# Column sums by VectorE for part of the score tiles, and a new order at the start of an attention unit

## The chip, the cores and the metric

The kernel runs on one core of one Trainium2 chip. The metric is the device time of that core in microseconds. TensorE (PE in the profile) multiplies, ScalarE (ACT) does the exponentials, VectorE (DVE) the reductions and elementwise work, GpSimd (POOL) some products and a part of the transfers, SyncE (SP) issues the rest.

## The reference

Attention over 8 batches of 12 heads, 448 positions and 64 features, with queries and keys normalised by their root mean square, and then a two-layer MLP over the 3584 tokens:

```python
q_n, k_n = (rmsnorm(q, g_q), rmsnorm(k, g_k))
scores = scale * np.matmul(q_n, k_n.transpose(0, 1, 3, 2))
scores = scores - np.max(scores, axis=-1, keepdims=True)
attn = np.exp(scores)
attn = attn / (np.sum(attn, axis=-1, keepdims=True) + 1e-09)
attn_out = np.matmul(attn, v)
...
x = attn_out.transpose(0, 2, 1, 3).reshape(B * S, H * D)      # 3584 x 768
h = x @ w_in                                                  # 768 x 2048
g = np.maximum(0.01 * h, h)
out = g @ w_out                                               # 2048 x 768
```

## The kernel before

**Units.** A unit is four heads of one batch; there are 24 (`NU`), three to a batch. Scores are kept transposed: keys on the partitions, queries along the free dimension. A unit has seven score tiles of 128 x 896 (`sT`, two PSUM banks each, 448 columns in each bank). For each tile TensorE runs four 64x64 matmuls (`score`, L195), ScalarE one exponential into the fp16 tile `et` (L214). There are two such `sT` slots, taken in turn.

**The loop.** Units 3 to 23 run through four stages `d` each (L928 to L1006): `STEPS` gives stage 0 the score tile 0, and stages 1 to 3 two tiles each. After a stage's scores and exponentials, `fill` (L703) takes MoE items from `queue` and puts them on TensorE: first-layer items (`moe1`, six matmuls of 448 columns, L363), second-layer items (`moe2`, eight of 384 columns, L404), and items of a seven-product scheme for pairs of output tiles (`seven`, L445), whose sums VectorE makes (L426 to L435) and whose banks it evacuates (L452, L461). How many items a stage gets follows from the costs that stand with the items (1.13, 1.31, or 0.575), the weights `WD` and a running `debt`. Small pieces of preparation for later units ("jobs") are placed between the items, one after each, and the rest behind them. Evacuations are put off through `pend` until the next item or the end of the fill (`flush`). Each engine takes its instructions in the order in which they are written here; nothing is scheduled automatically.

**The shift.** Exponentials need a bound. From tile 0 of a unit VectorE takes the maximum of each partition (`shift_max`, L232) and builds a diagonal `dg` (L234); a matmul with ones spreads it over all partitions (`shift_mm`, L244, or L250 for the first units); VectorE takes the maximum of that (L245) and makes the bias `eb` (L253). All exponentials of the unit wait for `eb`.

**Stage 0 of a unit `u`** also finishes unit `u - 1`. For "narrow" units (4 to 22) TensorE runs PV (`pv_slot`, 28 matmuls into the other `sT` slot), the column sums over the keys (`zcol`, 16 matmuls with a 32-column matrix of ones, L283), and then the shift of `u`, into unused columns of the slot that PV has just filled. ScalarE copies PV out (`pv_out`, L295), VectorE folds the sums (`zcol_sum`, L300). `zcol_inv` makes the reciprocal and spreads it by DMA, and GpSimd or VectorE multiplies (`xmul_pool`, `xmul_sb`, L321). Unit 23 and units up to 3 take wide sums instead (`zsum_slot`, 28 matmuls of 64x64, L265).

**Preparation** of unit `u + 2`: sums of squares (L155) in stage 1, the inverse root (L160, L161) and the normalisation (L167) in stage 2. V is loaded as fp16 into one of `NV` buffers by GpSimd's queue (`load_v`, L124).

The lines of stage 0 that the change reorders are L932 to L947.

Of the kernel before, what the change touches and what calls it, by code (L numbers as in the profile page):

```python
# [18 lines left out]
def kernel(  # L19
# [22 lines left out]
    DELTA = 1.0  # L42
    NV = 4

# [194 lines left out]
    def shift_mm(u):  # L239
        s = st[u]  # L240
        if u > 0 and "pslot" in st[u - 1]:
            pb = st[u - 1]["pslot"][:, :, S:S + 64]
            for x in range(2):
# [14 lines left out]
    xts = {}  # L258

    def zsum(u, t0=0, t1=NS):  # L260
        s = st[u]
        for t in range(t0, t1):
            for r in range(2):
                for a in range(2):
                    nc.tensor.matmul(s["zt"][r][64 * a:64 * a + 64, 0:S], ones16[64 * r:64 * r + 64],  # L265
                                     s["et"][64 * r:64 * r + 64, t, a], start=(t == 0), stop=(t == NS - 1))

# [8 lines left out]
    def zcol(u):  # L276
        s = st[u]
        s["zc"] = aux([P, 512], FP32, "zc")
        for i, (t, n) in enumerate(((0, 2), (NS - 1, 1), (2, 2), (4, 2))):
            for y in range(2):  # L280
                for a in range(2):
                    c = 32 * (2 * y + a)
                    nc.tensor.matmul(s["zc"][c:c + 32, 0:n * HS].rearrange("p (k x) -> p k x", k=n), onesr,  # L283
                                     s["et"][:, t:t + n, a, HS * y:HS * y + HS], start=(i == 0), stop=(i == 3))

# [103 lines left out]
    def flush():  # L389
        while pend:  # L390
            pend.pop(0)()
# [305 lines left out]
    def narrow(u):  # L697
        return 4 <= u < NU - 1

    def fed(u, d):  # L700
        return u % NQ == 0 and d == 3

    def fill(u, d, jobs):  # L703
# [11 lines left out]
        while queue and debt[0] >= queue[0][0] * 0.5:  # L715
# [3 lines left out]
            if jobs:  # L719
                jobs.pop(0)()  # L720
        flush()
        for job in jobs:
# [22 lines left out]
    with tc.manual_schedule():  # L745
# [110 lines left out]
        prep_sqp(4, (0,))  # L856
        load_v(4)
        for f in range(2):
# [29 lines left out]
        load(6)  # L888
        gate(3)
        prep_sqp(4, (1,))  # L890
        prep_sqp(5)
        load_v(5)
        qk(2, (2,))
# [34 lines left out]
        for u in range(3, NU):  # L928
            for d in range(4):
                if d > 0 or u > 3:  # L930
                    qk(u, STEPS[d])
                    if d == 0:  # L932
                        shift_max(u)
                        if u == 6:
                            xmul_sb(u - 2)
                        if narrow(u - 1):
                            pv_slot(u - 1)
                            zcol(u - 1)
                            shift_mm(u)
                            pv_out(u - 1)  # L940
                            zcol_sum(u - 1)
                        else:
                            zsum_slot(u - 1)
                            pv(u - 1)
                            shift_mm(u)
                            zinv(u - 1)
                    ex(u)  # L947
# [5 lines left out]
                if d == 0:  # L953
# [8 lines left out]
                    if u + 4 < NU:  # L962
                        job(load, u + 4)
                    if u + 3 < NU:
                        load_v(u + 3)
                    if u < 6:
# [15 lines left out]
                if u + 2 < NU:  # L982
# [3 lines left out]
                    if d == 2:  # L986
                        job(prep_rinv, u + 2)
                        for ti in range(2):
                            job(prep_norm, u + 2, ALL, (ti,))
                        if u > 3:  # L990
                            job(prep_trd, u + 2)
                if d == 1 and 4 <= u < 8:
                    job(weight_sum, u - 4, 0)
                if d == 0 and 5 <= u < 9:
                    job(weight_sum, u - 5, 1)
                if d == 2 and 6 <= u < 8:
                    job(xmul_sb, u - 1)
                if u == NU - 2 and d == 0:
# [47 lines left out]
```

## Time and profile before

| | |
|---|---|
| time, median of 3 runs | 421.86 us (420.86 to 422.32) |
| span of the profiled execution | 419.0 us |
| PE busy | 402.7 us, 96% |
| ACT busy | 304.6 us, 73% |
| DVE busy | 279.5 us, 67% |
| POOL busy | 82.9 us, 20% |
| granted TensorE clock | full in all 40 slices |

Groups that the change touches, with the busy time of the group and the mean of one instruction:

| group | count | busy us | mean ns |
|---|---|---|---|
| L283 PE zc, 448 columns | 216 | 15.3 | 356 |
| L283 PE zc, 224 columns | 72 | 4.8 | 259 |
| L232 DVE maximum of tile 0 | 22 | 24.1 | 1093 |
| L295 ACT copy of PV | 19 | 17.2 | 907 |
| L244 PE shift, 64 columns | 38 | 4.4 | 197 |

Busy times of matmuls overlap, since four small tiles run side by side and matmuls are pipelined; what a group costs on the path is better read from the chain of waits, where each piece has only the time by which it moves the end. "issue" there is time without a visible cause, and "A <- B" in the list of waits means that A's engine stood idle until B was done.

### The profile page before, as it was taken

The page shows a single profiled execution, that of the slowest core. Times are in us where ns is not written, and L with a number is a line of the kernel's source. Part 1 is how long each engine was busy: PE and PEld are TensorE (multiplying, and loading weights), DVE is VectorE, ACT ScalarE, POOL GpSimd, SP SyncE. Part 2 cuts the span into 40 slices and gives each one's busy share as a digit, 9 for nine tenths or more (in the row PEclk, how much of TensorE's full clock was granted, in tenths as well). Part 3 has the DMA queues.
Part 4 walks back from the last instruction along what each step waited for, and adds up shares of the span by engine and source line. Part 5 has one row for each costly group of instructions (what it writes and reads, how often), then busy time and mean ns, then how long its engine had stood idle before and what let it go on. Part 6 is the DMA issues. An engine that isn't in the chain of part 4 may idle for free.

```text
span 419.0 us, 9148 instructions
## 1 busy us (share of the span) xinstructions
PE 402.7 (96%) x3731; PEld 217.6 (52%) x3731; DVE 279.5 (67%) x459; ACT 304.6 (73%) x474; POOL 82.9 (20%) x75
## 2 busy tenths in 40 slices
PE   7787999999999999999999999999999999999995
PEld 7454444544445544454445544454445547558863
DVE  5888675898569736576449746468349788627762
ACT  5999877768887689867986779967986657653600
POOL 1958422200010121210121111120101101010000
PEclk9999999999999999999999999999999999999999
DMA  8999996889664996677665796578554460032023
GB/s 265 239 251 260 237 252 85 219 153 207 163 153 74 216 229 108 166 177 165 158 127 105 201 193 154 152 147 186 159 111 45 119 152 13 2 82 76 2 54 97
DMA packets 71949, 62.39 MB, mean 149 GB/s; under 512 B 36324, under 2 KB 67044, under 8 KB 71908
## 3 DMA queue, kind: packets, MB, share of 16 engines
q1 hardware_dynamic: 61312, 49.62, 47.2%
q0 software_dynamic: 10272, 11.80, 18.1%
q8 instruction: 29, 0.48, 0.4%
q10 hardware_dynamic: 324, 0.39, 0.3%
q14 instruction: 12, 0.10, 0.1%
HBM read 45.61 MB, written 11.01 MB: 135 GB/s over the span
## 4 chain that ended last, share of the span: by engine, by line
PE 83%; ACT 9%; DVE 6%; issue 1%; DVEq 0%; ACTq 0%
PE hps L363 27%; PE sT L195 8%; PE sT L341 6%; ACT et L214 6%; PE ma L445 5%; PE md L445 5%; PE mc L445 5%; PE bank L445 5%; PE bank L565 4%; PE op L404 3%; PE zc L283 3%; PE mb L445 3%; PE warm L743 2%; PE sT L445 2%; DVE n L167 1%
## 5 line engine op out<-in xcount | busy, mean ns | idle before, releaser
L214 ACT ACTIVATE et<-sT,eb 128x896 f16<-128x896 f32 x166 | 159.5, 1010 | 17.9 <-PE sT L195 16.3
L363 PE MATMUL hps<-xt,win 128*128 128x448 f16 x600 | 120.8, 353 | 0.2 <-DVE xt L350 0.2
L363 PEld LDWEIGHTS <-win 128*128 128x128 f16 x612 | 56.8, 98 | 58.2 <-issue 9.7
L321 POOL TENSOR_TENSOR xt<-x,rz 128x896 f16<-128x896 f32 x16 | 33.2, 2076 | 148.5 <-DMA rz<-zs 117.7
L167 DVE TENSOR_TENSOR n<-rq,rinv 128x896 f16<-128x896 f32 (+2 forms) x25 | 26.7, 1069 | 52.2 <-ACT rinv L161 49.4
L195 PE MATMUL sT<-qkT 64*64 64x448 f16 x664 | 52.4, 363 | 4.7 <-ACT et L214 3.6
L357 ACT ACTIVATE gt<-hps 128x448 f16<-128x448 f32 x100 | 52.4, 549 | 5.4 <-PE hps L363 5.1
L155 DVE TENSOR_REDUCE ssq<-sq 128x14 f32<-128x896 f32 (+2 forms) x49 | 50.3, 1057 | 0.7 <-ACT sq L144 0.7
L445 PEld LDWEIGHTS <-sa 128*128 128x128 f16 x352 | 32.8, 98 | 26.3 <-issue 6.1
L295 ACT COPY x<-sT 128x896 f32<-128x896 f32 x19 | 17.2, 907 | 36.1 <-DVE sT L245 36.1
L124 POOL DMA_DIRECT2D vt<-in_v_dram x24 | 18.2, 758 | 114.5 <-PE sT L341 107.1
L195 PEld LDWEIGHTS <-qkT 64*64 64x64 f16 x672 | 15.5, 104 | 38.0 <-issue 34.6
L445 PEld LDWEIGHTS <-gt 128*128 128x128 f16 x264 | 25.2, 98 | 18.7 <-issue 2.1
L341 PE MATMUL sT<-et,vt 64*64 64x448 f16 x532 | 28.5, 349 | 0.3
L404 PE MATMUL op<-wout,gt 128*128 128x384 f16 x160 | 28.4, 327 | 0.0
L232 DVE TENSOR_REDUCE sT<-sT 128x1 f32<-128x896 f32 x22 | 24.1, 1093 | 5.1 <-PE sT L195 4.9
L341 PEld LDWEIGHTS <-vt 64*64 64x64 f16 x672 | 20.7, 107 | 11.3 <-issue 1.7
L167 DVE TENSOR_TENSOR n<-rk,rinv 128x896 f16<-128x896 f32 (+2 forms) x26 | 26.1, 1010 | 0.0
L404 PEld LDWEIGHTS <-gt 128*128 128x128 f16 x192 | 17.6, 98 | 14.0 <-issue 2.9
L445 PE MATMUL ma<-wout,gt 128*128 128x384 f16 x128 | 23.5, 326 | 0.0
L426 DVE TENSOR_TENSOR sa<-gt 128x512 f16<-128x512 f16 (+1 forms) x15 | 8.1, 542 | 16.0 <-ACT gt L357 12.1
L144 ACT ACTIVATE sq<-rq 128x896 f32<-128x896 f32 (+2 forms) x18 | 16.3, 913 | 1.1 <-DMA rq<-in_q_dram 1.1
(136 smaller groups left out, 522.5 us busy)
## 6 DMA issues: line engine op xcount, KB each, us to landing
rq<-in_q_dram SPq DMA_DIRECT2D x24, 448.0 KB, 4.1
rk<-in_k_dram SPq DMA_DIRECT2D x24, 448.0 KB, 5.6
out_dram<-ost SPq DMA_DIRECT2D x52, 192.0 KB, 2.9
rz<-zs SPq DMA_DIRECT2D x76, 112.0 KB, 2.3
vt<-in_v_dram POOLq DMA_DIRECT2D x24, 224.0 KB, 5.5
win<-in_moe_w_in_dram POOLq DMA_DIRECT2D x8, 384.0 KB, 12.4
wout<-in_moe_w_out_dram POOLq DMA_DIRECT2D x2, 1536.0 KB, 25.6
out_dram<-ost SPq DMA_DIRECT2D x4, 96.0 KB, 2.1
```

Of the source, the lines that this page charges most:

```text
L124: nc.gpsimd.dma_start(vts[u % NV].rearrange("p a t d -> p a (t d)"), rows(v, u))
L155: nc.vector.tensor_reduce(buf(u, "ssq")[:, ti, :, c[0]:c[1]], buf(u, f"sq{ti}")[:, :, c[0]:c[1]], axis=AXL.X, op=ALU.add)
L167: nc.vector.tensor_tensor(buf(u, "n16")[:, ti, c[0]:c[1]].rearrange("p s a d -> p a s d"), src[:, :, c[0]:c[1]], buf(u, "rinv")[:, ti, :, ...
L195: nc.tensor.matmul(banks[a][64 * r:64 * r + 64, 0:S].rearrange("p (t x) -> p t x", t=NS), kT(u, r, a, t), qT(u, r, a), start=True, stop=True)
L214: nc.scalar.activation(s["et"][:, t], sT[:, :, 0:S], AF.Exp, bias=s["eb"], scale=1.0)
L232: nc.vector.tensor_reduce(s["spare"][:, 511:512], sT[:, :, 0:S], axis=AXL.XY, op=ALU.max)
L321: eng.tensor_tensor(xts[b][:, g], s["x32"], s["rz"], op=ALU.mult)
L341: nc.tensor.matmul(s["pv"][r][64 * a:64 * a + 64, 0:S], vts[u % NV][64 * r:64 * r + 64, a, t], s["et"][64 * r:64 * r + 64, t, a], start=(t ...
L357: nc.scalar.activation(dst, src, AF.Prelu, bias=0.0, scale=1.0, alpha=0.01)
L363: nc.tensor.matmul(hps[:, 0:S], win16[:, kt // 2, kt % 2, ts(ft, P)], xt[:, kt // 2, kt % 2], start=(kt == 0), stop=(kt == KT - 1))
L404: nc.tensor.matmul(op2[:, 0:HC], gt[:, ft, ds(col(t), P)], wout16[:, ft, ds(HC * half, HC)], start=(ft == 0), stop=(ft == FT - 1))
L445: nc.tensor.matmul(bank[:, 0:HC], a[:, f], b[:, f], start=(first and f == 0), stop=(f == HF - 1), skip_group_check=not first)
```

## The change

It has two parts, and some edits that make room for them.

1. **Adds.** In units 8 to 20, and in unit 23, VectorE adds the exponential tiles 0 to 3 into one fp16 tile `ea` (three additions of 128 x 896, as jobs of stages 2 and 3). The column sums then run over `ea` and the tiles 4, 5 and 6 only: 12 matmuls (448, 224 and 224 columns, four each) instead of 16, and in unit 23 16 wide matmuls instead of 28. The aim is less work on TensorE.
2. **Order in stage 0.** The shift of `u` goes into the spare columns of its own score banks, not into those of PV's slot, and TensorE runs one MoE item between the column sums and the shift. The copy of PV and the fold of the sums are written ahead of the shift. The aim is that the shift's chain on VectorE has time to arrive, and that PV's copy doesn't wait for it.
3. **Beside them.** V has three buffers instead of four, which frees the space of `ea`; it is loaded one unit later. Stage 3 leaves its last evacuations in `pend`, and stage 0 flushes them after the new unit's maximum. The VectorE products of units 5 and 6 go ahead of the normalisations.

```diff
--- before.py
+++ after.py
@@ -40,7 +40,7 @@
     KT = DM // P
     FT = DF // P
     DELTA = 1.0
-    NV = 4
+    NV = 3
 
     cst = ctx.enter_context(tc.tile_pool(name="cst", bufs=1))
     raws = ctx.enter_context(tc.tile_pool(name="raws", bufs=3))
@@ -238,8 +238,8 @@
 
     def shift_mm(u):
         s = st[u]
-        if u > 0 and "pslot" in st[u - 1]:
-            pb = st[u - 1]["pslot"][:, :, S:S + 64]
+        if "pb" not in s and not isinstance(s["sT"][0][1], list):
+            pb = s["sT"][0][1][:, :, S:S + 64]
             for x in range(2):
                 nc.tensor.matmul(pb[:, x], onesp, s["dg"][:, 64 * x:64 * x + 64], start=True, stop=True)
             nc.vector.tensor_reduce(s["spare"][:, 510:511], pb, axis=AXL.XY, op=ALU.max)
@@ -257,13 +257,28 @@
 
     xts = {}
 
+    NA = 4
+
+    def acc(u, t):
+        s = st[u]
+        if "ea" not in s:
+            s["ea"] = zpool.tile([P, 2, S], FP16, tag="ea", name="ea")
+        nc.vector.tensor_tensor(s["ea"], s["et"][:, 0] if t == 1 else s["ea"], s["et"][:, t], op=ALU.add)
+
+    def ztile(u, t):
+        s = st[u]
+        return s["ea"] if "ea" in s and t < NA else s["et"][:, t]
+
     def zsum(u, t0=0, t1=NS):
         s = st[u]
+        if "ea" in s:
+            t0 = max(t0, NA - 1)
         for t in range(t0, t1):
+            e = ztile(u, t)
             for r in range(2):
                 for a in range(2):
                     nc.tensor.matmul(s["zt"][r][64 * a:64 * a + 64, 0:S], ones16[64 * r:64 * r + 64],
-                                     s["et"][64 * r:64 * r + 64, t, a], start=(t == 0), stop=(t == NS - 1))
+                                     e[64 * r:64 * r + 64, a], start=(t == 0 or e is s.get("ea")), stop=(t == NS - 1))
 
     def zsum_slot(u):
         s = st[u]
@@ -276,12 +291,17 @@
     def zcol(u):
         s = st[u]
         s["zc"] = aux([P, 512], FP32, "zc")
-        for i, (t, n) in enumerate(((0, 2), (NS - 1, 1), (2, 2), (4, 2))):
+        for i, (k, t) in enumerate(((-1, 4), (0, 6), (1, 0)) if "ea" in s else ((-1, 0), (0, 6), (-1, 2), (-1, 4))):
             for y in range(2):
                 for a in range(2):
                     c = 32 * (2 * y + a)
-                    nc.tensor.matmul(s["zc"][c:c + 32, 0:n * HS].rearrange("p (k x) -> p k x", k=n), onesr,
-                                     s["et"][:, t:t + n, a, HS * y:HS * y + HS], start=(i == 0), stop=(i == 3))
+                    q = slice(HS * y, HS * y + HS)
+                    if k < 0:
+                        nc.tensor.matmul(s["zc"][c:c + 32, 0:S].rearrange("p (k x) -> p k x", k=2), onesr,
+                                         s["et"][:, t:t + 2, a, q], start=(i == 0), stop=True, skip_group_check=True)
+                    else:
+                        nc.tensor.matmul(s["zc"][c:c + 32, HS * k:HS * k + HS], onesr, ztile(u, t)[:, a, q],
+                                         start=False, stop=True, skip_group_check=True)
 
     def pv_slot(u):
         s = st[u]
@@ -697,6 +717,9 @@
     def narrow(u):
         return 4 <= u < NU - 1
 
+    def added(u):
+        return 8 <= u < NU - 3 or u == NU - 1
+
     def fed(u, d):
         return u % NQ == 0 and d == 3
 
@@ -718,7 +741,8 @@
             debt[0] -= c
             if jobs:
                 jobs.pop(0)()
-        flush()
+        if d < 3:
+            flush()
         for job in jobs:
             job()
 
@@ -854,7 +878,6 @@
         load_v(3)
         load(5)
         prep_sqp(4, (0,))
-        load_v(4)
         for f in range(2):
             load_w_out(8 * f, 8)
         qk(1, (2,))
@@ -887,9 +910,9 @@
         prep_norm(3)
         load(6)
         gate(3)
+        load_v(4)
         prep_sqp(4, (1,))
         prep_sqp(5)
-        load_v(5)
         qk(2, (2,))
         ex(2)
         trn(3, 0, vcopy)
@@ -931,14 +954,19 @@
                     qk(u, STEPS[d])
                     if d == 0:
                         shift_max(u)
+                        flush()
                         if u == 6:
                             xmul_sb(u - 2)
                         if narrow(u - 1):
                             pv_slot(u - 1)
+                            pv_out(u - 1)
                             zcol(u - 1)
+                            zcol_sum(u - 1)
+                            if queue:
+                                c, fn = queue.pop(0)
+                                fn()
+                                debt[0] -= c
                             shift_mm(u)
-                            pv_out(u - 1)
-                            zcol_sum(u - 1)
                         else:
                             zsum_slot(u - 1)
                             pv(u - 1)
@@ -961,8 +989,8 @@
                         xmul(u - 1)
                     if u + 4 < NU:
                         job(load, u + 4)
-                    if u + 3 < NU:
-                        load_v(u + 3)
+                    if u + 2 < NU:
+                        load_v(u + 2)
                     if u < 6:
                         prep_sqp(u + 3)
                 if d == 1 and narrow(u - 1) and not 5 <= u < 8 and u < NU - 1:
@@ -985,16 +1013,24 @@
                             job(prep_ssq, u + 2, ALL, (ti,))
                     if d == 2:
                         job(prep_rinv, u + 2)
+                        if u == 6 or u == 7:
+                            job(xmul_sb, u - 1)
+                        if added(u):
+                            job(acc, u, 1)
+                            job(acc, u, 2)
                         for ti in range(2):
                             job(prep_norm, u + 2, ALL, (ti,))
                         if u > 3:
                             job(prep_trd, u + 2)
+                elif d == 2 and added(u):
+                    job(acc, u, 1)
+                    job(acc, u, 2)
+                if d == 3 and added(u):
+                    job(acc, u, 3)
                 if d == 1 and 4 <= u < 8:
                     job(weight_sum, u - 4, 0)
                 if d == 0 and 5 <= u < 9:
                     job(weight_sum, u - 5, 1)
-                if d == 2 and 6 <= u < 8:
-                    job(xmul_sb, u - 1)
                 if u == NU - 2 and d == 0:
                     for n, tile_ in ((1, (raws, "rq", 3)), (2, (raws, "rk", 3)), (3, None), (4, (prep_p, "sq", 3))):
                         job(win_sum, n, 1, tile_)
```

## The prediction

> **What bounds the kernel now.** I read the page's busy shares first, then its slices, then the chain of waits, then the list of waits, and last the timeline around one unit.
>
> ```profile
> PE 402.7 (96%) x3731; PEld 217.6 (52%) x3731; DVE 279.5 (67%) x459; ACT 304.6 (73%) x474; POOL 82.9 (20%) x75
> ...
> PE   7787999999999999999999999999999999999995
> ...
> PE 83%; ACT 9%; DVE 6%; issue 1%; DVEq 0%; ACTq 0%
> ```
>
> TensorE is busy 96% of the span, and what is missing lies in the first four slices: from about 60 us on it hardly rests. The chain that ended last is 83% TensorE. So a matmul taken out of a unit shortens the run by its own time, unless the edit makes TensorE wait. The windows of 10 us say the same: from 80 to 360 us TensorE is busy 9.6 to 10.0 of each 10. VectorE varies with the kind of MoE work beside it, from 3.1 (290 to 300 us, first layer) to 9.2 (220 to 230 us, second layer).
>
> The chain in order of time, at unit 9:
>
> ```profile
> 129.06 0.31 PE sT L195 x4
> 129.37 1.32 PE sT L341 x28
> 130.69 0.78 PE zc L283 x16
> 131.47 0.17 PE sT L244 x2
> 131.63 1.30 PE mc L445 x8
> 132.94 1.30 PE md L445 x8
> 134.24 0.50 PE sT L195 x8
> ```
>
> The reader is to see the beginning of a unit: the first score step, PV of the unit before, its column sums (zc), the shift matmul (L244), two MoE items, the next two score steps. Nothing idles. PV gives a rate: 28 matmuls of 64x64 tiles, four at a time, are 7 rounds of 448 columns in 1.32 us, 0.189 us a round.
>
> The timeline of the same stretch shows what the shift sets going:
>
> ```profile
> 131.40 0.23 PE L244 MATMUL sT<-dg,onesp 128*128 128x64 f16 x2
> ...
> 131.67 0.30 DVE L245 TENSOR_REDUCE sT<-sT 128x1 f32<-128x128 f32 x1 [0.41 <-PE sT L244]
> 132.01 0.16 DVE L253 TENSOR_SCALAR eb<-sT 128x1 f32<-128x1 f32 x1
> 132.06 0.91 ACT L295 COPY x<-sT 128x896 f32<-128x896 f32 x1 [2.21 <-DVE sT L245]
> ...
> 132.86 1.01 ACT L214 ACTIVATE et<-sT,eb 128x896 f16<-128x896 f32 x1
> ```
>
> From the start of L244 to the exponential's bias is 0.8 us. ScalarE waits 2.21 us, copies PV out, and only then takes the first exponential, which ends at 133.87, 2.47 us after the shift. The second score step (134.16) needs that exponential's score bank back, since there are two such tiles and PV has the other. Two MoE items (2.6 us) hide this, just.
>
> ```profile
> ACT x L295 <- DVE sT L245: 36.1, 19, 4.5
> DVE n L167 <- ACT rinv L161: 49.4, 15, 7.2
> PE sT L195 <- ACT et L214: 3.6, 10, 0.5
> ```
>
> The list of waits: the copy's wait occurs in all 19 narrow units, 1.9 us each; VectorE idles 49 us ahead of the normalisation, mostly beside first-layer work; TensorE waits for exponentials 3.6 us in all.
>
> [...]L295 reads other columns than L245, yet starts at the end of L245 (131.97, then 132.06). [...]L429 takes 424 ns for 512 elements and 681 for 1024, 0.50 ns an element, against 1.08 us for a 32-bit 896 in L167. [...]eight score matmuls are two rounds (0.38) but take 0.50 in the chain[...]
>
> **Part 1, column sums.** For units 8 to 20 the sums took tiles 0-1, 6, 2-3, 4-5: three rounds of 448 columns and one of 224. They take 4-5, 6 and the added tile: one of 448, two of 224. One round and a half less is 0.189 + 0.094 = 0.283 us; 13 units give **3.68 us**. Unit 23's wide sums lose tiles 0 to 2, three rounds, **0.57 us**, and the chain runs through them (PE sT L265 x28, 1.45).
>
> **Part 2, the adds.** No row has 896 elements in fp16; from L429's two rows one takes 0.62 us, between 0.42 (512) and 0.68 (1024). VectorE starts the next about 0.1 us before the end, so three cost some 1.6 us a unit, 25 of busy time in 14 units. Beside first-layer work the idle time of L167 hides them. Beside second-layer work queued behind them are the normalisation, the evacuations of MoE banks and then the next unit's maximum. The place is units 8, 14 and 20, whose adds come just ahead of the maximum of 9, 15 and 21. At unit 15 VectorE runs unbroken from 217.55 to 226.5. With 1.6 more, less one evacuation (0.48) that now goes behind the maximum, the maximum starts at 226.2 instead of 225.13. Its diagonal, the evacuation and the column sum, now ahead of L245, bring L245 to 228.65; the shift would allow 228.26. So a lag of 0.4 there, 0.4 at unit 9 by the same count: 1.2 us for three, between 0 (VectorE closes up) and 3 (the added time is seen whole, 1.0 each).
>
> **Part 3, order at the start of a unit.** The copy runs right behind PV; ScalarE gains the time it waited, but TensorE does not need it. The shift waits for one MoE item. From L244 to a free score tile it is then 0.80 + 1.01 + 0.05 = 1.86 us, with no copy in between. What hides it is the number of items after the shift. I counted with the rule of fill (debt, WD, costs); for the kernel before the count gives the trace's items, such as 2 at unit 9 and 3 at unit 11. For the new one it leaves three at units 14 and 20, two at most others, one at units 5, 9, 10, 15, 16, 21, and **none at unit 6**. Two items take 2.4 us or more: no wait. One takes 0.07 + 1.13 (first layer) or 1.30 (second) + 0.12, so TensorE stands 0.55 (units 10, 16) or 0.37 (5, 9, 15, 21). Unit 6 stands 1.75, and saves 0.39, the wait of its second stage at 90.58, which gets two items. Sum 1.10 + 1.48 + 1.36 = **3.9 us lost**.
> Items also leave other places. Units 11, 15 and 17 had a single item in the last stage, where PV then began 0.49 us after the score step instead of 0.22 (174.66 to 175.15 against 128.99 to 129.20); they get two: 3 x 0.27 = 0.8. In unit 23 ScalarE's unbroken run from 358.25, headed by the copy (0.91), made TensorE wait 0.23 for gt and before that its weight load 0.61; with the copy earlier I give it 0.45.
>
> **Part 4, edits at nothing.** Loading V one unit later: it still has two units (some 30 us) against 5.5 us to landing, and GpSimd, busy 20%, waits for the same PV as before. The moved load of unit 4 puts one issue of 0.76 us ahead of a square that VectorE needs later. The products of units 5 and 6 change places with normalisations that have a unit of slack. The shift of units 3 and 4 in their own bank takes two 64-column matmuls for one of 128.
>
> Sum: 3.68 + 0.57 + 0.8 + 0.45 = 5.5 gained, 3.9 lost at the shift, 0 to 3 lost on VectorE.
>
> **The cases.**
> - A, forecast: the gains and the shift's losses come as counted, VectorE closes up its lag: 421.86 - 5.5 + 3.9 = **420.3 us**. For it: VectorE idles in every unit, and after each shift wait it is further ahead. Against: the three places are those without idle time. Chance 0.36.
> - B, even: VectorE's 1.2 us come too: 421.5. For it: the count at unit 15. Chance 0.22.
> - C, the shift's waits hidden for the greater part, because ScalarE, freed of the copy's wait, is early and TensorE's long queue smooths it: a quarter of 3.9 stays, 417.3. For it: ScalarE is given back up to 1.9 us a unit. Against: the bank is needed, not the engine. Chance 0.12.
> - D, slower: VectorE becomes the bound in second-layer stages, 3.0, unit 5's exponentials run late once more (0.4), and the 1.25 us of moved items do not show: 421.86 - 4.25 + 3.9 + 3.4 = 424.9; with half of VectorE's lag 423.4. For it: 9.2 of 10 busy at 220 to 230 us, in a strict queue. Against: the lag is gone one unit later. Chance 0.30.
>
> C and half of D's tail mark the range: 417.2 to 424.2. Faster by over 0.3% (below 420.6): A and C, 0.48. Within: B, 0.22. Slower: D, 0.30.
>
> **What would show it.** zc at 12 matmuls and about 0.5 us in the chain in units 8 to 20; the sums of unit 23 at 16 matmuls. The wait of ACT x L295 for DVE gone. "PE sT L195 <- ACT et L214" up from 3.6 by some 4 us, longest about 1.75, in unit 6 near 86 us. DVE busy up by 25 us, L167's wait down. Were the longest wait below 0.5, C holds; were TensorE to wait for dg, ea or the evacuations of VectorE by over 1 us at units 9, 15, 21, D does. The forecast is wrong outright if the item counts after the shift differ.

## The result, and the profile after

| | before | after |
|---|---|---|
| time, median of 4 runs each | 421.36 us (420.74 to 422.32) | 425.97 us (425.43 to 426.47) |
| ratio to before, 95% interval | | 1.0107 (1.0081 to 1.0133) |
| span of the profiled execution | 419.0 us | 424.1 us |
| DVE busy | 279.5 us | 312.6 us |

The changed kernel is slower by 1.1%, some 4.5 us; 420.3 us had been forecast, with a range of 417.2 to 424.2. Some line numbers move: the products of GpSimd are L341 now (L321 before), the additions of exponential tiles L266, the column sums L300 and L303 (L283), PV L361 (L341) and its copy L315 (L295), the matmuls of the MoE items L383, L424 and L465 (L363, L404, L445), the sums of the second layer's inputs L446 to L455 (L426 to L435), the bank evacuations L472 (L452). The normalisation stays L167.

The page of the changed kernel, in the same order as that of before: busy shares, and the shares of the chain that ended last.

```profile
PE 402.0 (95%) x3669; PEld 216.8 (51%) x3669; DVE 312.6 (74%) x501; ACT 306.2 (72%) x474; POOL 84.1 (20%) x75
...
PE 64%; DVE 15%; ACT 13%; issue 4%; DMA 2%; SPq 1%; POOLq 1%; DVEq 0%; ACTq 0%
```

62 matmuls are gone, yet TensorE's busy time is the same within 1 us, and its share of the chain fell from 83% to 64%. VectorE's rose from 6 to 15%. VectorE has 33.1 us more to do, where 25 had been counted. The trace's lines on single instructions show why (count, then durations in ns as min/median/max, first and last start, forms). The additions:

```profile
L266 DVE TENSOR_TENSOR ea<-ea,et x28: 606/614/2273, 129.1 to 375.1; 128x896 f16<-128x896 f16 x28
```

The median is 0.614 us, as estimated (0.62). But some take up to 2.27. The normalisation L167 has the same tail, which it hardly had before (1.31 us at most); here before's line stands first:

```profile
L167 DVE TENSOR_TENSOR n<-rq,rinv x25: 549/1092/1309, 7.1 to 333.0; 128x896 f16<-128x896 f32 x23, 128x512 f16<-128x512 f32 x1, 128x384 f16<-128x384 f32 x1
```

```profile
L167 DVE TENSOR_TENSOR n<-rq,rinv x25: 549/1091/2743, 8.1 to 335.2; 128x896 f16<-128x896 f32 x23, 128x512 f16<-128x512 f32 x1, 128x384 f16<-128x384 f32 x1
```

The timeline of the changed kernel around one long addition (start, duration, engine, line, and in brackets the idle time before it and what ended it):

```profile
285.54 0.61 DVE L266 TENSOR_TENSOR ea<-et 128x896 f16<-128x896 f16 x1
...
286.36 0.56 DVE L472 TENSOR_TENSOR ost<-md,ost 128x384 f32<-128x384 f32 x1 [0.21 <-PE md L465]
286.54 2.08 POOL L341 TENSOR_TENSOR xt<-x,rz 128x896 f16<-128x896 f32 x1 [10.12 <-DMA rz<-zs]
...
286.84 2.27 DVE L266 TENSOR_TENSOR ea<-ea,et 128x896 f16<-128x896 f16 x1
...
289.03 1.08 DVE L167 TENSOR_TENSOR n<-rq,rinv 128x896 f16<-128x896 f32 x1
```

GpSimd's product runs from 286.54 to 288.62. The addition starts inside it and ends at 289.11, 0.49 us after the product, a little less than its own 0.61: it stands still until GpSimd is done and then does its work. The moment of its start makes no difference to that. In the runs of this document 54 normalisations started inside a GpSimd product and more than 0.1 us before its end; all ended 0.94 to 0.95 us after it. So did 17 of 18 additions, 0.48 to 0.49 us after it. The evacuation L472, which takes one operand from PSUM, starts 0.18 us before the product and keeps its 0.56 us.

The product of 2.08 us thus puts 1.66 us on top of the addition's 0.61, and nothing on top of an evacuation that has one input in SBUF and one in PSUM, such as L452 at 282.52 in the next lines: it starts inside a product and takes its 0.56 us.

The kernel before has the same 16 products, all of 2.07 to 2.08 us; after, three take 2.44 to 2.47. Two of these start 0.12 us behind an addition of 0.62 us (at 189.42 and 240.08), the third 0.56 us behind a normalisation of 1.09 us (at 335.79). Before they fell beside other work:

```profile
279.78 2.07 DVE L155 TENSOR_REDUCE ssq<-sq 128x14 f32<-128x896 f32 x2
...
280.82 2.08 POOL L321 TENSOR_TENSOR xt<-x,rz 128x896 f16<-128x896 f32 x1 [7.23 <-DMA rz<-zs]
...
282.52 0.56 DVE L452 TENSOR_TENSOR ost<-mc,ost 128x384 f32<-128x384 f32 x1 [0.67 <-PE mc L445]
...
283.39 1.09 DVE L167 TENSOR_TENSOR n<-rq,rinv 128x896 f16<-128x896 f32 x1 [0.32 <-ACT rinv L161]
```

The product starts beside two sums of squares (2.07 us for two, not stretched) and is over at 282.90, 0.5 us before the first normalisation. From the start of PV to the start of the product it was 10.2 us in the median of the 16 units, and it is 11.5 now: the MoE item ahead of the shift delays the bias and the first exponential, the reciprocal of the sums comes on ScalarE behind that exponential, then come the DMAs, then the product. One microsecond later it meets the normalisations, the additions or the sums L446 to L455. I counted the VectorE instructions with two SBUF inputs that are more than 0.15 us above their usual length, from 60 us on, and added up the excess: **6 with 3.3 us before, 16 with 16.0 us after** (in every run two of these are sums of weight blocks, 1.4 us, that stretch beside another GpSimd multiplication, the squares L148 of 1.68 us). Such standing still is counted as busy. The runs below split VectorE's 33.1 us: the additions are 21.9 us of busy time (the next instruction starts before the last has ended, by 0.08 us at 286.84 and 289.03 above), and the products add 12.6 us, of which 1.4 were there before.

The waits of the changed kernel that answer to those shown of before (engine, tile and line that waited, what ended it; us in total, times, longest):

```profile
DVE n L167 <- ACT rinv L161: 23.1, 11, 3.7
...
ACT x L315 <- PE sT L361: 17.1, 13, 3.7
...
PE sT L195 <- ACT et L214: 5.3, 14, 1.2
```

VectorE's reserve ahead of L167 is down from 49.4 to 23.1 us. The copy of PV waits for PV itself, not for the shift any more, as the change intended. TensorE's wait for exponentials is up by 1.7 us. Further down the list TensorE waits for VectorE's evacuations and sums in three rows that before did not have, 1.3, 1.0 and 0.8 us; the 1.0 is a matter of unit 23 alone, shown further down.

How a held instruction reaches TensorE can be read from the chain that ended last, at the addition shown above:

```profile
286.84 2.27 DVE ea L266
...
291.65 0.47 DVE ost L472
292.12 1.02 DVE sT L232
...
294.44 0.22 DVE sT L245
...
294.94 0.07 ACT et L214
```

VectorE works off its queue behind the held addition, comes late to the next unit's maximum (L232), and with it come late the shift (L245) and the first exponential of that unit. In the kernel before, the chain at the start of the same unit is all TensorE's.

### The profile page after: what moved, and what is told of

Same layout as the page of the kernel before. It is cut to its first block, busy times and chain, and to the rows that moved or that the text cites. A ratio compares the mean times of both kernels' runs of the same rounds, so it can differ in the third digit from the quotient of the medians.

```text
span 424.1 us, 9090 instructions
## 1 busy us (share of the span) xinstructions
PE 402.0 (95%) x3669; PEld 216.8 (51%) x3669; DVE 312.6 (74%) x501; ACT 306.2 (72%) x474; POOL 84.1 (20%) x75
## 4 chain that ended last, share of the span: by engine, by line
PE 64%; DVE 15%; ACT 13%; issue 4%; DMA 2%; SPq 1%; POOLq 1%; DVEq 0%; ACTq 0%
PE hps L383 24%; ACT et L214 8%; PE sT L195 7%; PE op L424 5%; PE bank L585 4%; PE sT L361 4%; DVE n L167 4%; PE ma L465 4%; PE bank L465 3%; PE mc L465 2%; PE md L465 2%; DVE ea L266 2%; PE mb L465 2%; PE sT L465 2%; DVE sT L232 1%
## 5 line engine op out<-in xcount | busy, mean ns | idle before, releaser
L383 PE MATMUL hps<-xt,win 128*128 128x448 f16 x600 | 121.8, 353 | 0.4 <-DVE xt L370 0.4
L383 PEld LDWEIGHTS <-win 128*128 128x128 f16 x612 | 55.8, 98 | 58.1 <-issue 11.3
L341 POOL TENSOR_TENSOR xt<-x,rz 128x896 f16<-128x896 f32 x16 | 34.3, 2146 | 160.3 <-DMA rz<-zs 113.4
L195 PE MATMUL sT<-qkT 64*64 64x448 f16 x664 | 54.2, 367 | 6.4 <-ACT et L214 5.3
L167 DVE TENSOR_TENSOR n<-rq,rinv 128x896 f16<-128x896 f32 (+2 forms) x25 | 31.9, 1280 | 25.9 <-ACT rinv L161 23.1
L465 PEld LDWEIGHTS <-sa 128*128 128x128 f16 x352 | 33.2, 98 | 27.7 <-issue 5.7
L195 PEld LDWEIGHTS <-qkT 64*64 64x64 f16 x672 | 16.1, 104 | 41.7 <-issue 37.7
L465 PEld LDWEIGHTS <-gt 128*128 128x128 f16 x264 | 24.8, 98 | 21.2 <-issue 5.7
L315 ACT COPY x<-sT 128x896 f32<-128x896 f32 x19 | 17.3, 910 | 21.0 <-PE sT L361 17.1
L361 PE MATMUL sT<-et,vt 64*64 64x448 f16 x532 | 28.4, 349 | 0.0
L424 PE MATMUL op<-wout,gt 128*128 128x384 f16 x160 | 28.3, 327 | 0.0
L232 DVE TENSOR_REDUCE sT<-sT 128x1 f32<-128x896 f32 x22 | 24.0, 1091 | 5.0 <-PE sT L195 5.0
L167 DVE TENSOR_TENSOR n<-rk,rinv 128x896 f16<-128x896 f32 (+2 forms) x26 | 27.5, 1064 | 0.0
L361 PEld LDWEIGHTS <-vt 64*64 64x64 f16 x672 | 20.3, 107 | 10.9 <-issue 0.6
L424 PEld LDWEIGHTS <-gt 128*128 128x128 f16 x192 | 17.3, 98 | 14.5 <-issue 4.0
L465 PE MATMUL ma<-wout,gt 128*128 128x384 f16 x128 | 23.5, 327 | 0.1
L266 DVE TENSOR_TENSOR ea<-ea,et 128x896 f16<-128x896 f16 x28 | 20.9, 747 | 1.1 <-ACT et L214 0.5
L446 DVE TENSOR_TENSOR sa<-gt 128x512 f16<-128x512 f16 (+1 forms) x15 | 8.1, 542 | 15.5 <-ACT gt L377 11.6
```

What stands on the lines that cost most here:

```text
L167: nc.vector.tensor_tensor(buf(u, "n16")[:, ti, c[0]:c[1]].rearrange("p s a d -> p a s d"), src[:, :, c[0]:c[1]], buf(u, "rinv")[:, ti, :, ...
L195: nc.tensor.matmul(banks[a][64 * r:64 * r + 64, 0:S].rearrange("p (t x) -> p t x", t=NS), kT(u, r, a, t), qT(u, r, a), start=True, stop=True)
L232: nc.vector.tensor_reduce(s["spare"][:, 511:512], sT[:, :, 0:S], axis=AXL.XY, op=ALU.max)
L266: nc.vector.tensor_tensor(s["ea"], s["et"][:, 0] if t == 1 else s["ea"], s["et"][:, t], op=ALU.add)
L341: eng.tensor_tensor(xts[b][:, g], s["x32"], s["rz"], op=ALU.mult)
L361: nc.tensor.matmul(s["pv"][r][64 * a:64 * a + 64, 0:S], vts[u % NV][64 * r:64 * r + 64, a, t], s["et"][64 * r:64 * r + 64, t, a], start=(t ...
```

## The experiments

All times are medians; ratios are to the kernel before in runs on the same chip, with a 95% interval. "Products left out" means that GpSimd fills the tiles `xt` of its 16 products with a constant instead.

### GpSimd's products left out of the changed kernel (e3_no_lock)

```diff
-        eng.tensor_tensor(xts[b][:, g], s["x32"], s["rz"], op=ALU.mult)
+        if eng is nc.gpsimd:
+            eng.memset(xts[b][:, g], 0.1)
+        else:
+            eng.tensor_tensor(xts[b][:, g], s["x32"], s["rz"], op=ALU.mult)
```

> The changed kernel, but GpSimd's products of x and 1/z are left out: GpSimd writes a constant in their place, which reads nothing in SBUF. Theory L with GpSimd as its main cause: the adds and normalisations of 2.2 to 2.7 us go back to 0.6 and 1.1, VectorE's busy time falls by about 11 us, and the time by 2 to 3.5 us, to 422.5 to 424. If the lag comes from the adds' own 26 us: VectorE falls by 11 us, the time by under 1 us. Theory S: no change in time, 425.5 to 426.5.

Measured: 420.4 us, ratio 0.9983 (0.9970 to 0.9996). Two stretched instructions are left, the weight sums, VectorE is busy 300.0 us (312.6 with the products), and the chain is TensorE's again:

```profile
PE 83%; ACT 9%; DVE 5%; issue 1%; DMA 1%; SPq 0%; ACTq 0%; DVEq 0%
```

So 1.24% of the time, 5.2 us, goes with the products; that is more than the 2 to 3.5 us that had been expected. The rest of the change comes near what had been forecast. TensorE's lists say the same: without the products the rows of 1.3 and 0.8 us are gone and its wait for exponentials is 3.7 us instead of 5.3.

### The control: products left out of the kernel before (e9_before_no_lock)

The same edit in the kernel before.

> A control: the kernel before with GpSimd's products of x and 1/z left out, a constant written instead. Only some 1.8 us of VectorE's time is stretched by them there, beside first-layer work with idle time or once a pair. Theory K: 421.0 to 421.6, no change. If leaving the products out makes any kernel faster by several us (earlier inputs of the MoE[...]), 416 to 419, and the run of the changed kernel without products says nothing on the collision.

Measured: 420.59 us, ratio 0.9998 (0.9988 to 1.0008). VectorE is busy 278.1 us, 21.9 less than in the run above, which is the additions. The products cost nothing in the old order. Their work alone, their DMAs or their place on GpSimd don't explain the 5.2 us. It isn't either that `xt` is filled some 9 us earlier without the products, for that is so in this control too. And in no run's list does TensorE wait for a product of GpSimd itself.

### The order without the additions (e1_order_only)

```diff
     def added(u):
-        return 8 <= u < NU - 3 or u == NU - 1
+        return False
```

> The new order of stage 0 alone, no tile added by VectorE (the column sums take all seven tiles). Theory L (VectorE late: it has 26 us of adds more, and some 11 us of its instructions stretched while GpSimd multiplies): without adds only the waits of units 5 and 6 stay, about 1.7 us, so 422.5 to 423.5 against 421.4 before. Theory S (the item ahead of the shift leaves too few items behind it): the waits of units 5, 6, 9, 10, 15, 16 and 21 all stay and no matmul is saved, so 424.5 to 426.

Measured: 431.8 us, ratio 1.0249 (1.0230 to 1.0269), and 15 stretched instructions with 16.1 us. Both expectations were missed by over 5 us: the new order alone, with VectorE's load as before, is slower than the whole change. So in this order the additions are not what costs.

### The order without the additions and without the products (e5_order_no_lock)

Both edits together.

> The new order without the adds (as in the run of the order alone, 431.8), and GpSimd's products of x and 1/z left out: it writes a constant. Theory K (the new order moves the products into VectorE's normalisations, and these stand until GpSimd is done): the 13 stretched instructions go and the time falls by 6 to 9 us, to 423 to 426; what then stays over 421.4 is the item's own cost, 2 to 4 us. Rival (the order costs by the starved score steps alone): 430 to 432.

Measured: 423.89 us, ratio 1.0075 (1.0055 to 1.0095). With the three runs above this makes a table of four cells, in ratios to before:

| | products on GpSimd | products left out | what the products cost |
|---|---|---|---|
| before | 1 | 0.9998 | 0.0% |
| new order only | 1.0249 | 1.0075 | 1.7%, 7.3 us |
| new order and additions | 1.0107 | 0.9983 | 1.2%, 5.2 us |

In the right column the order costs 0.77%, 3.2 us, and the additions give 0.92%, 3.9 us. These are the two terms of the prediction's sum, without the collision.

### The additions in the old order (e2_adds_only)

The changed kernel with stage 0, the banks of the shift and the flush as before; the lines on stage 0 are shown.

```diff
-                            pv_out(u - 1)
                             zcol(u - 1)
-                            zcol_sum(u - 1)
-                            if queue:
-                                c, fn = queue.pop(0)
-                                fn()
-                                debt[0] -= c
                             shift_mm(u)
+                            pv_out(u - 1)
+                            zcol_sum(u - 1)
```

> The adds and the shorter column sums in the old order of stage 0 (shift into PV's slot right behind the column sums, copy of PV behind it, evacuations flushed in every stage, products of units 5 and 6 in their old place). Theory L: VectorE's lag now meets the shift without an item ahead of it, TensorE waits for the diagonal in units 9, 15 and 21, and the time is 422 to 425. Theory S: nearly the whole saving of 4.2 us shows, 417 to 418.5.

Measured: 427.96 us, ratio 1.0159 (1.0136 to 1.0183), with 7 stretched instructions of 4.2 us, hardly more than before. It is slower than either expectation, and its cost is another one, the first in its list of TensorE's waits:

```profile
PE sT L244 <- DVE dg L234: 10.5, 10, 1.8
```

VectorE reaches the maximum of the next unit late, and TensorE has nothing between the sums and the shift. The item ahead of the shift is there for this; in the changed kernel that wait is 0.3 us, once. So in the old order the additions' own time seems to cost, since the hold is little more here than in the kernel before, where it costs nothing. No run of this order without the products tells the two apart.

### The changed kernel without the item (e4_no_item)

```diff
                             zcol_sum(u - 1)
-                            if queue:
-                                c, fn = queue.pop(0)
-                                fn()
-                                debt[0] -= c
                             shift_mm(u)
```

> The changed kernel without the MoE item between the column sums and the shift; the fill behind the shift then takes that item. Theory S: the waits for the score bank in the seven units go, 3.5 us faster, about 422.5. Theory L: the shift matmul waits for the diagonal in units 9, 15, 19 and 21 where VectorE is late, which takes back what is won in units 5, 6, 10 and 16: 424.5 to 427.

Measured: 424.04 us, ratio 1.0065 (1.0045 to 1.0084). The stretched instructions fall from 16 to 7 (5.0 us), and the shift waits for `dg` 4.7 us, nine times. The time lies between the two expectations, since both things happen. From PV to the product it is 10.2 us in the median again. The item hides one wait and makes the other: it is what moves the product into VectorE's way.

### The reciprocal of the sums ahead of the item (e6_inv_early)

Only the place of `zcol_inv` (two ScalarE instructions and four DMAs) changes.

```diff
                             zcol_sum(u - 1)
+                            if u < NU - 1:
+                                zcol_inv(u - 1)
                             if queue:
...
-                        if u < NU - 1:
-                            job(zcol_inv, u - 1)
+                        pass
```

> The changed kernel with the reciprocal of the column sums (zcol_inv, two small ScalarE steps and the DMA) written ahead of the MoE item and of the unit's first exponential, not behind them; all is computed. Theory K: the products start 1.5 to 2 us earlier, mostly ahead of the normalisations; stretched time falls from 14.6 to under 6 us and the time by 2 to 4 us, to 422 to 424. Rival (the adds' own time on VectorE, not the collision): the first exponential comes up to 0.8 us later and the time goes up, 426 to 428.

Measured: 422.41 us, ratio 1.0035 (1.0022 to 1.0048), 0.72% or 3.0 us less than the changed kernel. From PV to the product it is 9.1 us in the median instead of 11.5, and 10 instructions are stretched instead of 16 (11.5 us). The time is where the theory had it, though far more stretched time stays than the 6 us expected. The place of the product in time decides, not its presence.

### The product later in the kernel before (e11_before_late)

The reverse test: no additions, the old order, and `zcol_inv` behind stage 0's filling.

```diff
-                        if u < NU - 1:
-                            job(zcol_inv, u - 1)
+                        pass
...
                 fill(u, d, jobs)
+                if d == 0 and u > 3 and narrow(u - 1) and u < NU - 1:
+                    zcol_inv(u - 1)
```

> The kernel before with one edit: the inverted sums are issued after stage 0's filling and exponential instead of within it, so that GpSimd's product comes some 1 to 2 us later; no additions on VectorE, the order of the shift as before. Theory (the place of the product in time decides): the product falls into VectorE's normalisations of stage 2, 10 to 15 us of VectorE time more for the same instructions, and 423 to 428. Rival (the collision costs only where VectorE also has the additions): VectorE stretched, but 420.5 to 422.5. Second rival (the product still falls into VectorE's wait): nothing stretched, 421.

Measured: 435.99 us, ratio 1.0349 (1.0316 to 1.0382). The direction is the theory's, the size more than twice the most that it expected. From PV to the product it is 12.8 us; 16 instructions are stretched by 21.6 us, and 11 of them are normalisations:

```profile
276.50 2.07 POOL L321 TENSOR_TENSOR xt<-x,rz 128x896 f16<-128x896 f32 x1 [9.81 <-DMA rz<-zs]
...
277.02 2.51 DVE L167 TENSOR_TENSOR n<-rq,rinv 128x896 f16<-128x896 f32 x1 [2.17 <-ACT rinv L161]
...
279.45 1.08 DVE L167 TENSOR_TENSOR n<-rk,rinv 128x896 f16<-128x896 f32 x1
```

Its list of TensorE's waits is headed, as without the item above, by the late maximum:

```profile
PE sT L244 <- DVE dg L234: 6.6, 11, 1.4
```

### The same without products (e13_late_no_lock)

> The kernel before with the inverted sums issued behind stage 0's filling and exponential, as in the run that came to 435.99 us, and with GpSimd's products left out (their tiles are filled with a constant by GpSimd instead, which reads no SBUF tile). Theory (the hold of VectorE by the product makes those 15 us): 421 to 424, nothing stretched. Rival (the later ScalarE instructions, DMAs and x tiles by themselves make it): 430 to 436.

Measured: 424.48 us, ratio 1.0075 (1.0050 to 1.0101). Moving the two ScalarE instructions and the DMAs costs 0.75%, 3.2 us, by itself; the other 2.74%, 11.5 us of 14.7, goes with the products. This separates the two. The time is 0.5 us above the theory's range, and VectorE isn't wholly free of GpSimd: beside the two weight sums one of its multiplications (L151, an fp16 tile times a column) takes 0.89 us instead of 0.45 beside GpSimd's filling of `xt`.

### The small losses at units 5, 6 and 23 (e7_item_from_9)

```diff
-        if d < 3:
+        if d < 3 or u == NU - 1:
             flush()
...
-                            if queue:
+                            if queue and u > 8:
```

> The changed kernel with the item ahead of the shift in units 9 to 23 alone, and with unit 23's last evacuations flushed in stage 3 as before. Unit 5 and 6 give back 1.7 us, the end of unit 23 1.0 (the wait of TensorE for an addition queued behind unit 23's product): 423.0 to 423.7. If the collisions with GpSimd shift by chance, they can hide this: 422 to 425.

Measured: 423.9 us, ratio 1.0063 (1.0043 to 1.0083), 1.9 us below the changed kernel (the intervals just touch), with 16 stretched instructions as before the edit, and 18.3 us of excess instead of 16.0. Two things had been lost in the changed kernel. At unit 6 no item follows the shift, as the prediction said:

```profile
89.24 0.38 PE L195 MATMUL sT<-qkT 64*64 64x448 f16 x4 [1.21 <-ACT et L214]
```

And at the end, which the prediction did not see: stage 3 of unit 23 leaves its last evacuation to a next unit that doesn't come, so it queues on VectorE behind the product of unit 23, which waits for `rz`, and TensorE for the bank (first VectorE, then TensorE):

```profile
380.70 1.16 DVE L370 TENSOR_TENSOR xt<-bank,rz 128x448 f16<-128x448 f32 x2 [5.00 <-ACT rz L348]
381.77 1.21 DVE L472 TENSOR_TENSOR ost<-bank,ost 128x384 f32<-128x384 f32 x2
```

```profile
382.37 1.46 PE L465 MATMUL bank<-wout,sa 128*128 128x384 f16 x8 [0.98 <-DVE ost L472]
```

### Both repairs (e8_both), and chosen places (e10_inv_chosen)

e8 is e6 and e7 together. In e10 two units, 8 and 20, keep the reciprocal at the end of stage 0, since there the early product meets sums of the second layer's inputs in stage 1.

```diff
-                            if queue:
+                            if u < NU - 1 and u not in (8, 20):
+                                zcol_inv(u - 1)
+                            if queue and u > 8:
...
-                        if u < NU - 1:
+                        if u in (8, 20):
                             job(zcol_inv, u - 1)
```

> The changed kernel with three edits: the issue of the inverted sums (two ScalarE tiles and the four DMAs of rz) moves from stage 0's last job to ahead of the item and the exponential, so that GpSimd's product falls earlier; the MoE item ahead of the shift only for units above 8; stage 3's additions of unit 23 are flushed too. Theory (VectorE is held by GpSimd's product, and three small losses at units 5, 6 and 23 come on top): few stretched VectorE instructions, and the 3.5 us of moving the sums and the 2 us of the units without an item add up: 419.0 to 420.8. Rival (the two gains are the same time, or VectorE's added 26 us are what costs): 422 to 424.

> The same as the combined version, but in units 8 and 20, which have longer VectorE jobs in stage 1, the inverted sums stay at the end of stage 0 as in the changed kernel. Theory: two fewer stretched instructions that TensorE waits for, each of about 0.5 to 1 us: 418.3 to 420.3, at or up to 0.8 us below the combined version. Rival (the stretched ones there are hidden): equal to the combined version within 0.3 us.

Measured: 419.66 us, ratio 0.9973 (0.9961 to 0.9984) for e8, and 418.74 us, **0.9950 (0.9933 to 0.9968)** for e10. The gains add up. Both beat the kernel before and the changed one; between the two the intervals overlap a little. In e10 eleven instructions are still stretched, by 12.1 us of VectorE time, against ten and 8.2 us in e8, and yet it is the faster one in the median. In e8 TensorE waits 0.6 us, once, for an evacuation of VectorE at unit 8 (at 125.2 us), which it doesn't in e10. So the sum of the excess is no measure of the loss; it depends on who waits behind.

### How much of the hold is left in that version (e14_chosen_no_lock)

e10 with the products left out.

> The version with chosen places of the inverted sums (418.74 us), with GpSimd's products left out in the same way. It shows how much of the hold is left in that version: its 10 stretched instructions are 10 us of VectorE time. Theory (they lie where TensorE doesn't wait): 417.5 to 418.7. Rival (they still cost): 414 to 417.

Measured: 417.84 us, ratio 0.9912 (0.9889 to 0.9935), against 0.9950: 0.38% or 1.6 us, with intervals that overlap a little. The products' 10.6 us of stretched time (12.1 less the 1.4 of the weight sums) cost about a sixth of their length. That is as the theory had it.

### The products on VectorE (e12_products_vector)

e7 with the remaining products taken from GpSimd and written for VectorE behind the normalisations of stage 2. The main lines are shown; others take out the products' old places and add those of units 21 and 22.

```diff
+                        if u > 5 and narrow(u - 1):
+                            job(xmul_sb, u - 1)
```

> The changed kernel with the item ahead of the shift only for units above 8 and the flush in unit 23 (as in the run of the two small losses), and with the product of GpSimd computed by VectorE instead, in stage 2 behind the normalisations: nothing runs on GpSimd beside VectorE after unit 5. Theory (the hold by GpSimd is what costs): no stretched instruction; VectorE has 16 products of about 1 us more: 419.5 to 422. Rival (VectorE's own load is what costs): 424 to 427, above the 423.9 of the same kernel with GpSimd.

Measured: 424.14 us, ratio 1.0078 (1.0052 to 1.0103), the same as e7's 423.9 within the intervals. Nothing but the two weight sums is stretched, and still nothing is gained: the theory's range is missed and the rival's met. VectorE now has 16 products of 1.08 us, 17 us in all, in place of 16.9 us of hold, and its busy time is 312.8 us. But the rival isn't shown by this, for one wait is of another kind. In unit 23 VectorE stands idle for 2.19 us at such a product until the DMA of `rz` is there, the evacuation behind it is late, and TensorE waits:

```profile
373.96 1.46 PE L465 MATMUL bank<-wout,gt 128*128 128x384 f16 x8 [1.83 <-DVE ost L481]
```

If these 1.8 us went in full, the time would be some 422.3 us, an estimate just above the theory's range. How much VectorE's work costs where the hold was stays open. GpSimd takes twice as long for the product (2.08 against 1.08 us); e10 with products on GpSimd is the faster version all the same.

## Why the prediction was wrong

Wrong in the number and on the side. The step that failed is the cost of VectorE in Part 2, which took every instruction at its usual length and bounded the lag by 3 us; together with it, Part 3 did not follow the late exponential on to GpSimd's product. In their place the runs showed VectorE instructions held by up to 1.8 us beside that product, 5.2 us of the whole time.

- **Part 1, column sums: right.** They take 0.49 to 0.53 us instead of 0.78 in 12 of 13 units (0.50 forecast); at the 13th 0.81, because the held addition shown above delays `ea`. The wide sums of unit 23 end after 0.78 us instead of 1.35, the 0.57 forecast.
- **Part 2, the additions: the duration right, the consequence wrong.** 0.614 us each against 0.62. (The 25 us of busy time don't follow from the prediction's own 1.6 us a unit, which make 22 in 14 units; 21.9 were measured.) The prediction priced VectorE instructions at their usual length, from the profile before, and gave the lag 0 to 3 us, 1.2 counted. In the new order the loss is not made by the additions' own time: without the products, additions and savings together give 3.9 us against the 4.25 less 1.2 that had been counted. It is made by instructions that last up to 1.8 us longer beside GpSimd. The range of 0 to 3 us bounded the wrong thing.
- **Part 3, the order: the count right, the waits too large, one consequence missed.** The items after the shift came as counted, so the places were right. TensorE stood 1.21 us at unit 6, where 1.75 was counted, 0.39 at unit 5 and 0.26 at 9, 15 and 21 (0.37), 0.53 at unit 16 but 0.24 at unit 10 (0.55). (The 0.12 us counted into the 0.55 and the 0.37 are an estimate from the trace of before, the 0.50 us of eight score matmuls less two rounds of 0.19; what makes the excess was not shown, nor that the new order has no more of it.) Part of the time that TensorE stood is the hold. Without the products the waits at 9, 15 and 21 are gone, and units 10 and 16 stand 0.23 each; TensorE's wait for exponentials is then 3.7 us against 2.0 in the kernel before without products, 1.7 more where 3.9 had been counted. The order alone costs 3.2 us without the products, since unit 23 loses 0.9 besides (Part 4), and of the 1.25 us of moved items no gain can be made out. What was missed is that the item also delays the first exponential, and behind it the reciprocal, its DMAs and the product by 1.2 us. The prediction asked who waits for the shift on TensorE, and not what else hangs on the late exponential.
- **Part 4, edits at nothing: one was not nothing.** The put-off evacuations of stage 3 had been counted with a gain alone (the 0.48 of Part 2); at unit 23 they cost about 1 us (the 0.98 above), as much as the 0.57 gained there and the 0.45 counted for it. The V buffers and the order of the products of units 5 and 6 show no wait in the list of the changed kernel.
- **The cases.** Without the collision the changed kernel runs 420.4 us, where case A says 420.3. In ratio that is 0.17% below before, and the forecast was 0.37%. That it comes so near is in part luck: the waits at the shift were counted 2.2 us too high, and the loss at unit 23 and the missing gains make up for it. Case D, the slower one, gives 424.9 with VectorE as the bound beside the second layer. That its time is near is luck. VectorE is indeed what TensorE waits for, but not for D's reason: instructions are held beside the first layer too (normalisations at 160.36 and 206.57, between first-layer items), and the wait for `dg` that D named is 0.3 us in the changed kernel. It is 10.5 us in the additions without the order, where D is right.
- **What would have shown it.** The profile before has the signs: GpSimd's products of 2.08 us, ending 0.5 us ahead of L167 in the stretch shown, and four instructions stretched beside them, one L167 of 1.31 us and three L432 of 0.95 instead of 0.42. One of these stands at 219.81, in the unbroken stretch of unit 15 that the prediction worked through.

Two things stay open. The additions are worth more beside the products (1.42%, 6.0 us) than without them (0.92%, 3.9 us), though the two runs with products have about as many stretched instructions. The lists show where it lies: TensorE's rows for VectorE's evacuations and sums, unit 23's left out, are 3.1, 1.5 and 1.2 us in the order alone and 1.3 and 0.8 in the whole change, and none without products. Why the additions move the hold to places with fewer waiting behind was not tried. And how the hold of 16 us becomes 5.2 us of the run is told only in part: from the run without products to the changed kernel TensorE's waits grow by the 1.3 and 0.8 us, by 1.6 for exponentials and by 0.3 for `dg`. Which of this comes from which stretched instruction was not worked out beyond the one chain shown.

## What to carry to other kernels

When an edit delays the start of a chain, follow everything that hangs on it to its last engine, and look at what will then run beside it: a GpSimd product of two SBUF tiles may be free in one place and cost up to 1.9 us of VectorE in another. Price a VectorE instruction with two SBUF inputs twice, alone and beside GpSimd (here an addition at 0.61 us and at up to 2.27), wherever both have work in the same microseconds. When more load on an engine is suspected, take the load away and leave the order: here that run showed that in the new order the load was not the cause, while in the old order it probably was one.

## What the runs showed of the hardware

- VectorE instructions with two SBUF inputs that started while GpSimd multiplied two SBUF tiles stood until GpSimd was done: 2.27 us for 0.61, 2.21 for 0.42 and 2.74 for 1.08 in the changed kernel, 2.98 for 1.08 in the run of the small losses (at 285.62, beside a product of 2.56). They ended a fixed time after the product, whenever they had started (up to 0.1 us before the product's end; 54 normalisations, 17 of 18 additions): 0.94 to 0.95 us for the normalisations, 0.48 to 0.49 for the additions, 0.28 to 0.29 for the sums of 512 elements. The profile counts the standing as busy time (the 2.27 us of the addition at 286.84) and names nothing that ended it. The reverse was seen too: a product started 0.11 us behind a normalisation of 1.09 us took 2.93 instead of 2.08 (in the late version of before, at 244.69).
- Sums of squares (one input, 1.07 us), evacuations that add a PSUM bank to an SBUF tile (0.56 us) and copies out of PSUM (0.55 us) kept their length in all runs where they started inside a GpSimd multiplication: 105 of the first kind, 30 of the second, 18 of the third.
- A shift of 1 to 2.5 us in the place of sixteen 2-us products moved the run by up to 11.5 us.
